# RWKV-6 attention and a SiLU MLP on one core: where block loads and one sum of weights stand in their queues

## The chip, the core and the metric

The kernel runs on one core of a Trainium2 chip. Such a core has a matrix engine (PE, TensorE), whose weight loads are shown apart as PEld, and a vector engine (DVE), a scalar engine (ACT), a general engine (POOL, GpSimd) and SyncE (SP), which here only issues transfers. Each engine takes its instructions in the order in which the program has them; an instruction whose semaphores are not yet set holds everything behind it on the same engine. The transfers themselves are carried out by 16 DMA engines.

The metric is the device time of one execution in microseconds. Before the change: 651.31 us, the median of 11 runs (649.45 to 654.97).

## The reference

A recurrent attention over 768 tokens, for 4 batches and 8 heads of 48 channels, and then a two-layer MLP on all 3072 tokens:

```python
for t in range(S):
    cur = np.einsum('bhd,bhe->bhde', u[None] * kt, vt)
    y[:, :, t] = np.einsum('bhd,bhde->bhe', rt, state + cur)
    state = wt[:, :, :, None] * state + np.einsum('bhd,bhe->bhde', kt, vt)
...
x = attn_out.transpose(0, 2, 1, 3).reshape(B * S, H * D)      # 3072 x 384
h = x @ w_in                                                  # 384 x 2048
g = h * (1.0 / (1.0 + np.exp(-h)))
out = g @ w_out                                               # 2048 x 384
```

r, k, v, w and u are 32-bit floats. The two weight matrices come as 64-bit floats, so that the kernel has to round them to 32 bits itself.

## The kernel before

**Units.** The sequence is cut into 6 chunks of 128 tokens, and the 4 batches into 2 pairs: 12 units, each 128 tokens of two batches. They are numbered from 0 in the code, so the third unit is `i = 2`, the fourth `i = 3`, the fifth `i = 4` and the sixth `i = 5`. A unit's attention is worked out in a tree of seven levels: at each level PE multiplies grown queries with grown keys (`score_products`, L527), VectorE copies the valid part into `score` under a mask (`keep_masked`, L537), and POOL and VectorE grow keys and queries for the next level (L491, L473, L595). Then the scores times the values give y (`y`, L665), the state is brought forward (`update`, L679 to L693), and y becomes x, the MLP's input (`dense_x`, L703 and L705, for the first two units, and `move_x`, ten transfers, later). A unit's MLP runs beside the attention of the units that follow it: eight `up` products with a Silu on ScalarE (L756, L762), then the product with w_out, plain for unit 0 (`down`, L775), and for the rest as seven products of halves (`quarter`, L819) with fewer multiplications, which need sums of the activations (`sums`, L801) and four sums of blocks of w_out, made once (`weight_sums`, L793). The last of these sums, `weight_sums(3)`, writes a block of w_out in place; the sixth of the seven products of unit 1 is its first reader.

**Loads of a unit.** The tokens of unit `i` stand in slot `i % 2` of `raw`. From the third unit on they come by `load_blocks` (L106): for each of w, k and r four calls, and each call issues four transfers of 32 tokens (16 or 32 KB), which makes 48 transfers for a unit. `load_values` (L119, L126) issues five more, `load_rk` (L90) four. All are issued by SyncE. The third unit's blocks are read first when VectorE transposes them (`turn`, L338).

**The diagonal.** A token's own term is not in the tree. POOL multiplies r, k and u (`bonus`), VectorE sums (`bonus_sum`, L415 and L419), and for `i >= 2` four small transfers on SyncE's queue put these sums into another order (`diag`, L425). ScalarE copies them (`bonus_spread`, L441 and L443), and VectorE writes them into `score` (L450).

**Rounding the weights.** The weights come in 16 pieces of 768 KB, 0 to 7 of w_in and 8 to 15 of w_out (`load_weight`, L178), into rooms that are used several times; pieces 0 to 5 are loaded at the start. The load of a later piece is issued right after the `join_weight` that has emptied its room: load 6 after piece 0, load 7 after piece 1, and so on to load 11 after piece 5; load 12 after piece 8, to load 15 after piece 11. A piece takes two steps on ScalarE for its upper bits (`head_weight`, L195 and L197), one for its lower ones into the buffer `p_w` (`tail_weight`, L203), two on VectorE (`join_weight`, L214 and L215) and a sum on POOL (`add_weight`, L227). The order of all this is written out by hand, in lists of steps that `do` emits one after the other. In the first of these, the second unit's tree begins beside the first unit's MLP; the third unit's blocks stand in it in three groups of four calls (`blocks[0:4]` is w, `[4:8]` k, `[8:12]` r).

**From the fourth unit on** the order comes from `mix(i)`: fourteen groups of steps of the attention, with the steps of the MLP of earlier units put between them (`ROOM` says how many behind each group). `mix` also deals out the loads for unit `i + 2`, with the values of unit `i + 1` in their middle, to the groups from the fourth on. For the fourth unit the loop adds `weight_sums(3)` at the end of group 4, which is the first burst of products (`burst`) and the masked copies of its first level (`keep_level`). The diagonal's four transfers stand in group 9 (`bonus_sum(i, 1)`), before `load_rk`.

Of the kernel before, what the change touches and what calls it, by code (L numbers as in the profile page):

```python
# [38 lines left out]
def kernel(  # L39
# [11 lines left out]
    nc = tc.nc  # L51
# [16 lines left out]
    NTOK = 2  # L68
# [650 lines left out]
    def both(fn, i, *args):  # L719
        return [(fn, i, b, *args) for b in range(NB)]  # L720

    def block_loads(i):
        return [(load_blocks, i, name, g) for name in "wkr" for g in range(4)]

    def mix(i):

        groups = [[*both(turn, i, "w"), (product, i, 0)],
                  [*both(turn, i, "k"), *both(turn, i, "r"), (odd_ones, i)], [(start_levels, i), (prepare_keys, i, 1)],
                  [(prepare, i, 1), *[(product, i, l) for l in range(1, NL)]],
                  [(burst, i, 1), (keep_level, i, 1)], [(keep_level, i, 2), (go_on, i, 2)],  # L730
                  [(prepare, i, 3), (reverse_v, i), (bonus, i, 0)],
                  [(burst, i, 3), (keep_level, i, 3), (bonus_sum, i, 0), (bonus, i, 1), (bonus, i, 2)],
                  [(keep_level, i, 4), (go_on, i, 4)],
                  [(prepare, i, 5), (bonus_sum, i, 1)] + ([(load_rk, i + 1)] if i + 1 < len(units) else []),
                  [(burst, i, 5), (keep_level, i, 5)], [(keep_level, i, 6), (go_on, i, 6), (bonus_spread, i), (bonus_write, i)],
                  both(turn_k, i), [*both(y_state, i), *both(y, i), *both(update, i), (move_x, i)]]

        loads = block_loads(i + NSLOT) if i + NSLOT < len(units) else []
        if i + 1 < len(units):
            loads.insert(len(loads) // 2, (load_values, i + 1))  # L740
        behind = groups[3:]
        for at, group in enumerate(behind):
            group += loads[at * len(loads) // len(behind):(at + 1) * len(loads) // len(behind)]
        return groups
# [89 lines left out]
    def ups(i):  # L834

        steps = [[(up, i, m)] for m in range(FC // 2)]
        for m in range(FH // 2 - 1):

            steps[FH // 2 + 1 + m].append((sums, i, m))
        steps[-1].append((sums, i, FH // 2 - 1))  # L840
        return steps

    def downs(i):
        return [[(quarter, i, x)] for x in range(7)]

    def do(*steps):
        for fn, *args in steps:
            fn(*args)
# [7 lines left out]
    def back(fn, i, *args):  # L856
# [8 lines left out]
    blocks = block_loads(2)  # L865
    others = {1: [(clear, 0), (beat, 6)], 2: [(turn, 1, 0, "r"), (head_weight, 0), (beat, 2)],
              3: [(turn, 1, 1, "r"), (head_weight, 1), (beat, 2)], 4: [(turn, 1, 1, "w"), (reverse_v, 0)],
              5: [(bonus_spread, 0), (bonus_write, 0), (turn, 1, 0, "w")], 6: [*both(turn_in, 1, "k"), *blocks[0:4], (tail_weight, 0)]}
    for l in range(1, NL):
        do((scores, 0, l), *[(grow_keys, 0, l + 1)] * (l + 1 < NL), *others[l])  # L870

    do((bonus, 1, 0), (bonus, 1, 1), (bonus, 1, 2), *both(y, 0), (turn_apart, 0), (join_weight, 0), (add_weight,),
       *blocks[4:8], (product, 1, 0), (tail_weight, 1), (turn, 1, 0, "k"), (join_weight, 1), (dense_x, 0, 0), (turn, 1, 1, "k"),
       (dense_x, 0, 1), (grow_queries, 1, 0), (odd_ones, 1), (tail_weight, 2), *both(turn_k, 0), (head_weight, 2),
       *blocks[8:12], (start_keys, 1, nc.gpsimd, True), (add_weight,), (up, 0, 0), (join_weight, 2),
       (start_keys, 1, nc.gpsimd, False), (add_weight,), (tail_weight, 3), (odd_keys, 1, 1), (head_weight, 3), (grow_keys, 1, 1),
       (scores, 1, 1, (join_weight, 3)), (add_weight,), (up, 0, 1), (tail_weight, 4), (grow_keys, 1, 2), (head_weight, 4),
       (up, 0, 2))


    others = {1: [], 2: [(bonus_sum, 1, 0), (bonus_sum, 1, 1), (load_rk, 2), *both(update, 0)],
              3: [(bonus_spread, 1), (reverse_v, 1), (clear, 1), (load_values, 2)]}

    def piece(i):
# [3 lines left out]
    for m in range(1, 4):  # L888
# [7 lines left out]
    blocks = block_loads(3)  # L896

    others = {0: [(up, 1, 1), (down, 0, 0, 0), *both(turn, 2, "k"), (product, 2, 0), (product, 2, 1)],
              1: [(up, 1, 2), *both(turn, 2, "r"), *[(product, 2, l) for l in range(2, NL)], *blocks[0:3]],
              2: [(down, 0, 0, 1), (odd_ones, 2), (start_keys, 2, nc.gpsimd, True), (grow_queries, 2, 0), *blocks[3:6]],  # L900
              3: [(up, 1, 3), (start_keys, 2, nc.gpsimd, False), (reverse_v, 2), *blocks[6:9]], 4: [(level, 2, 1), (up, 1, 4), *blocks[9:12]],
              5: [(down, 0, 0, 2), (up, 1, 5), (weight_sums, 0)]}
# [5 lines left out]
    blocks = block_loads(4)  # L908
# [10 lines left out]
    for i in range(3, len(units)):  # L919
        steps = downs(i - 2) + ups(i - 1)  # L920
        groups = mix(i)
        if i == NTOK + 1:

            groups[4].append((weight_sums, 3))
        for group, room in zip(groups, ROOM):
            do(*group)
            for step in steps[:room]:
                do(*step)
            steps = steps[room:]
# [32 lines left out]
```

## Time and profile before

| what | us |
|---|---|
| median of 11 runs | 651.31 |
| the profiled execution, and its span | 654.97, 653.2 |
| PE busy | 642.1 (98%) |
| PE weight loads busy | 580.8 (89%) |
| VectorE busy | 433.3 (66%) |
| POOL busy | 283.3 (43%) |
| ScalarE busy | 203.6 (31%) |
| PE busy from 28 to 70 us | 39.49 of 42.00 |
| PE busy from 140 to 150 us | 8.46 of 10.00 |
| PE busy from 150 to 183 us | 31.95 of 33.00 |
| PE busy from 183 to 234 us | 51.00 of 51.00 |

An entry of the page such as "L762 ACT ACTIVATE gt<-p_h" names the line of the code, the engine, the operation, and the tile written and the one read. In the timelines the first column is the start in us from the beginning of the span, the second the duration; what stands in square brackets is the idle time before it and what ended that. In the table of waits, the columns are the total in us, the number of waits and the longest. The clock is what the throttle granted to PE, 1.00 being full speed. The ends of matmuls are modelled, so that a busy PE isn't always a PE at its peak.

### The profile page before, as it was taken

How to read it: one execution, taken by the hardware profiler on the slowest of the kernel's cores; microseconds unless marked ns; L12 is line 12 of the kernel's file. 1: busy time of each engine (PE TensorE's matmuls, PEld its weight loads, DVE VectorE, ACT ScalarE, POOL GpSimd, SP SyncE). 2: the span in 40 equal slices, each digit the busy share in tenths (PEclk: the TensorE clock that was granted, in tenths of full speed). 3: DMA queues.
4: the chain of work that ended last, by engine and by line, in shares of the span. 5: the costliest groups of instructions: out<-in, count | busy, mean ns of one | idle time of the engine just before them, and what ended most of it. 6: DMA issues, size and time to landing. Idle time of an engine off the chain costs nothing.

```text
span 653.2 us, 12887 instructions
## 1 busy us (share of the span) xinstructions
PE 642.1 (98%) x4878; PEld 580.8 (89%) x4878; DVE 433.3 (66%) x737; ACT 203.6 (31%) x408; POOL 283.3 (43%) x356
## 2 busy tenths in 40 slices
PE   8999899999999999999999999999999999999998
PEld 7888776798899899899899899899989989989997
DVE  7879579888296586586686576586667765752031
ACT  5797782221221330331231231232222132131120
POOL 6898288565135334434416416416406505510000
PEclk9999899999999999999999999999999999999999
DMA  9956864544444513513513523432441022000000
GB/s 210 290 92 165 215 176 49 92 80 48 87 81 66 98 34 64 98 28 57 107 26 58 99 35 51 82 62 49 75 74 38 25 50 49 26 3 25 25 0 25
DMA packets 201134, 49.21 MB, mean 75 GB/s; under 512 B 188912, under 2 KB 195952, under 8 KB 201072
## 3 DMA queue, kind: packets, MB, share of 16 engines
q1 hardware_dynamic: 199488, 47.79, 36.0%
q8 instruction: 39, 0.64, 0.4%
q10 hardware_dynamic: 1584, 0.59, 0.4%
q14 instruction: 23, 0.19, 0.1%
HBM read 39.52 MB, written 4.72 MB: 68 GB/s over the span
## 4 chain that ended last, share of the span: by engine, by line
PE 90%; DMA 3%; SPq 2%; ACT 2%; DVE 1%; issue 1%; POOL 0%; POOLq 0%; ACTq 0%; DVEq 0%
PE p_h L756 35%; PE p_o L819 30%; PE p_sc L527 6%; PE p_m L527 4%; PE p_m L665 3%; PE p_m L775 3%; PE p_m L652 3%; PE p_m L350 2%; DMA w_out_sb<-in_moe_w_in_dram 1%; SPq L106 1%; PE p_m L639 1%; DMA w_out_sb<-in_moe_w_out_dram 1%; PE p_sc L679 1%; PE p_m L854 1%; PE p_m L703 1%
## 5 line engine op out<-in xcount | busy, mean ns | idle before, releaser
L756 PE MATMUL p_h<-xt,w_in_sb 128*128 128x256 f32 x1152 | 258.5, 382 | 1.8 <-ACT gt L762 1.1
L756 PEld LDWEIGHTS p_h<-xt,w_in_sb 128*128 128x128 f32 x1152 | 215.8, 190 | 33.8 <-ACT gt L762 1.3
L762 ACT ACTIVATE gt<-p_h 128x512 f32<-128x512 f32 x93 | 55.4, 596 | 222.6 <-PE p_h L756 222.4
L491 POOL TENSOR_TENSOR tk<-tk,tw 128x256 f32<-128x256 f32 x144 | 103.5, 742 | 21.9 <-ACT tk L461 15.0
L537 DVE COPY_PREDICATED score<-mask,p_sc 128x512 f32<-128x512 int8 x78 | 64.1, 885 | 60.4 <-PE p_sc L527 60.1
L819 PE MATMUL p_o<-w_out_sb,gt 128*128 128x192 f32 x528 | 90.5, 328 | 0.8 <-DVE w_out_sb L793 0.8
L819 PE MATMUL p_o<-own,temps 128*128 128x192 f32 x528 | 90.3, 328 | 0.7 <-DVE temps L828 0.7
L819 PEld LDWEIGHTS p_o<-own,temps 128*128 128x128 f32 x528 | 85.8, 190 | 2.1 <-DVE temps L828 1.0
L819 PEld LDWEIGHTS p_o<-w_out_sb,gt 128*128 128x128 f32 x528 | 85.8, 190 | 2.0 <-DVE w_out_sb L793 1.1
L684 POOL TENSOR_TENSOR state<-state,tw 128x512 f32<-128x512 f32 x16 | 19.7, 1253 | 119.7 <-PE p_m L652 119.7
L386 POOL TENSOR_TENSOR tw<-tw 128x256 f32<-128x256 f32 (+6 forms) x83 | 37.9, 456 | 56.6 <-DVE tw L338 52.7
L801 DVE TENSOR_TENSOR temps<-gt 128x256 f32<-128x256 f32 x88 | 44.1, 501 | 21.4 <-ACT gt L762 21.4
L461 ACT COPY tk<-tk 128x256 f32<-128x256 f32 x60 | 24.7, 412 | 81.5 <-PE p_sc L527 37.0
L527 PEld LDWEIGHTS p_sc<-tr,tk 48*128 48x128 f32 x640 | 39.2, 186 | 12.1 <-issue 8.4
L473 DVE TENSOR_TENSOR tr<-tr,tw 128x512 f32<-128x512 f32 x53 | 45.6, 861 | 3.3 <-POOL tk L491 1.1
L527 PE MATMUL p_sc<-tr,tk 48*128 48x128 f32 x640 | 47.1, 285 | 0.7 <-POOL tk L491 0.6
L408 POOL TENSOR_TENSOR ruk<-tokens_rk 128x768 f32<-128x768 f32 x10 | 18.6, 1861 | 66.7 <-DVE own_sums L415 66.7
L595 DVE TENSOR_TENSOR tr<-tr,tw 128x512 f32<-128x512 f32 x29 | 39.3, 1355 | 1.3
L537 DVE COPY_PREDICATED score<-mask,p_m 128x512 f32<-128x512 int8 x54 | 35.4, 706 | 0.0
L819 PE MATMUL p_o<-w_out_sb,temps 128*128 128x192 f32 x176 | 30.4, 326 | 0.0
L507 POOL TENSOR_TENSOR tk<-tk,tw 128x128 f32<-128x128 f32 x44 | 29.3, 701 | 1.7 <-ACT tk L497 1.7
L597 ACT COPY tr<-tr 128x512 f32<-128x512 f32 x29 | 18.4, 636 | 36.7 <-DVE tr L473 35.8
(144 smaller groups left out, 740.7 us busy)
## 6 DMA issues: line engine op xcount, KB each, us to landing
w_out_sb<-in_moe_w_in_dram SPq DMA_DIRECT2D x6, 768.0 KB, 7.1
tokens_rk<-in_r_dram SPq DMA_DIRECT2D x20, 192.0 KB, 3.4
tokens_rk<-in_k_dram SPq DMA_DIRECT2D x20, 192.0 KB, 3.9
w_out_sb<-in_moe_w_out_dram SPq DMA_DIRECT2D x4, 768.0 KB, 6.9
own<-in_moe_w_out_dram SPq DMA_DIRECT2D x4, 768.0 KB, 8.8
xt<-yt SPq DMA_DIRECT2D x60, 48.0 KB, 2.0
raw<-in_w_dram SPq DMA_DIRECT2D x80, 32.0 KB, 2.3
raw<-in_k_dram SPq DMA_DIRECT2D x80, 32.0 KB, 2.4
```

The costliest lines, as they stand in the source:

```text
L386: engine.tensor_tensor(out=up, in0=t[:, :, 0::2], in1=t[:, :, 1::2], op=ALU.mult)
L461: nc.scalar.copy(out=keys(i, X[(l + 1) % 2] * L + c, [4 * c, blocks], [c, 2], [1, c]), in_=keys(i, NP * L + c, [4 * c, blocks], [NP * L + ...
L473: nc.vector.tensor_tensor(out=odd, in0=odd, in1=tw[i][l][:, :, 0::2][:, :, :, None].to_broadcast([128, Q, L >> (l + 1), c]), op=ALU.mult)
L491: nc.gpsimd.tensor_tensor(out=out, in0=have, in1=odd_products(i, l, b, *blocks), op=ALU.mult)
L507: engine.tensor_tensor(out=keys(i, X[1] * L + 3 * b, [4, n], [1, 1]) if own else have, in0=have, in1=odd_products(i, 0, b, [4, n], skip=2 ...
L527: nc.tensor.matmul(bass.AP(tensor=s_p.tensor, offset=s_p.offset, ap=[s_p.ap[0], [apart * L // 2, 2], [1, L // 2]]), lhsT=tk[i][rows, X[l % ...
L537: nc.vector.copy_predicated(out=dst, mask=masks[l][:, :, None].to_broadcast([128, NB, NP, ni, c]), data=sc[e].rearrange("p (b q) (i c) -> ...
L595: nc.vector.tensor_tensor(out=new[:, :, :, 1, :], in0=old[:, :, :, 1, :], in1=tw[i][l][:, :, 0::2][:, :, :, None].to_broadcast([128, Q, L ...
L756: nc.tensor.matmul(p_h[:, a, :], lhsT=w_in_sb[:, c, f * 128:(f + 1) * 128], rhs=xt[i][:, c, :], start=(c == 0), stop=(c == KC - 1))
L762: nc.scalar.activation(out=gt[i, m], in_=p_h, func=AF.Silu)
L801: nc.vector.tensor_tensor(out=out, in0=one, in1=two, op=op)
L819: nc.tensor.matmul(p, lhsT=left(f), rhs=right[:, f, :], start=(f == 0), stop=(f == FH - 1))
```

## The change

Nothing is computed differently, and no instruction is added or dropped; three things change their place.

- The third unit's k blocks move from behind the first `add_weight` to behind `join_weight(2)`, and its r blocks from there to behind `up(0, 3)` in the first round of the loop over `m` below (`others[1]`).
- For the fourth unit alone (`i = 3`, `NTOK` is 2) the loads for the sixth unit and the values of the fifth are dealt out to the groups from number 10 on, where it was number 3.
- `weight_sums(3)` is put in as the second step of group 4, between the burst and the masked copies, where it was the last.

```diff
         loads = block_loads(i + NSLOT) if i + NSLOT < len(units) else []
         if i + 1 < len(units):
             loads.insert(len(loads) // 2, (load_values, i + 1))
-        behind = groups[3:]
+
+        behind = groups[3 if i > NTOK + 1 else 10:]
         for at, group in enumerate(behind):
             group += loads[at * len(loads) // len(behind):(at + 1) * len(loads) // len(behind)]
         return groups
...
     do((bonus, 1, 0), (bonus, 1, 1), (bonus, 1, 2), *both(y, 0), (turn_apart, 0), (join_weight, 0), (add_weight,),
-       *blocks[4:8], (product, 1, 0), (tail_weight, 1), (turn, 1, 0, "k"), (join_weight, 1), (dense_x, 0, 0), (turn, 1, 1, "k"),
+       (product, 1, 0), (tail_weight, 1), (turn, 1, 0, "k"), (join_weight, 1), (dense_x, 0, 0), (turn, 1, 1, "k"),
        (dense_x, 0, 1), (grow_queries, 1, 0), (odd_ones, 1), (tail_weight, 2), *both(turn_k, 0), (head_weight, 2),
-       *blocks[8:12], (start_keys, 1, nc.gpsimd, True), (add_weight,), (up, 0, 0), (join_weight, 2),
+       (start_keys, 1, nc.gpsimd, True), (add_weight,), (up, 0, 0), (join_weight, 2), *blocks[4:8],
        (start_keys, 1, nc.gpsimd, False), (add_weight,), (tail_weight, 3), (odd_keys, 1, 1), (head_weight, 3), (grow_keys, 1, 1),
...
-    others = {1: [], 2: [(bonus_sum, 1, 0), (bonus_sum, 1, 1), (load_rk, 2), *both(update, 0)],
+    others = {1: blocks[8:12], 2: [(bonus_sum, 1, 0), (bonus_sum, 1, 1), (load_rk, 2), *both(update, 0)],
               3: [(bonus_spread, 1), (reverse_v, 1), (clear, 1), (load_values, 2)]}
...
         if i == NTOK + 1:
 
-            groups[4].append((weight_sums, 3))
+            groups[4].insert(1, (weight_sums, 3))
```

## The prediction

> **What bounds the kernel now.** I began with the engine shares and the slices of the page.
>
> ```profile
> PE 642.1 (98%) x4878; PEld 580.8 (89%) x4878; DVE 433.3 (66%) x737; ACT 203.6 (31%) x408; POOL 283.3 (43%) x356
> PEclk9999899999999999999999999999999999999999
> ```
>
> TensorE (PE) is the bound; from 183 us its busy time in the table of stretches is 51.00 of every 51 us, so nothing is left there. What can be won lies in PE's idle time before 183 us, and in slice 5 (65 to 82 us), the one with a lower clock. Next, the waits of PE itself, longest first:
>
> ```profile
> PE p_m L665 <- ACT score L556: 2.3, 1, 2.3
> ...
> PE p_h L756 <- ACT gt L762: 1.1, 1, 1.1
> PE p_o L819 <- DVE w_out_sb L793: 0.8, 1, 0.8
> ...
> PE p_o L819 <- DVE temps L828: 0.7, 1, 0.7
> ```
>
> To see what is behind the first, ScalarE's timeline and SyncE's (start, duration, what):
>
> ```profile
> 60.94 1.48 ACT L365 COPY raw<-zero 128x1536 f32<-128x1536 f32 x1
> 67.06 0.90 ACT L195 ACTIVATE temps<-w_out_sb 128x768 bf16<-128x768 bf16 x1 [4.64 <-DMA w_out_sb<-in_moe_w_out_dram]
> ...
> 70.13 0.75 ACT L556 COPY score<-p_sc 64x256 f32<-64x256 f32 x2
> ```
> ```profile
> 39.65 0.38 SPq L178 DMA_DIRECT2D w_out_sb<-in_moe_w_in_dram  x1
> 40.14 10.13 SPq L106 DMA_DIRECT2D raw<-in_k_dram  x16
> 50.38 0.39 SPq L178 DMA_DIRECT2D w_out_sb<-in_moe_w_in_dram  x1
> 50.81 8.63 SPq L106 DMA_DIRECT2D raw<-in_r_dram  x16
> 59.97 0.90 SPq L178 DMA_DIRECT2D w_out_sb<-in_moe_w_out_dram  x2
> ```
>
> Weight load 8 (counting from 0) is issued at 59.97 and lands at 67.03, because loads 7 and 8 stand behind 16 block transfers each. Their rooms had long been free: DVE's L215 of piece 1 ended at 35.81, of piece 2 at 39.22. ScalarE waits 4.64 us in order, the copy of the score behind it is late, and PE stands from 68.28 to 70.54. The idle time isn't its whole price; the granted clock (the column after busy time) in half-microsecond stretches:
>
> ```profile
> 70.50:71.00 0.50, 0.46 (x8) 1.00 1.30 227
> ...
> 72.50:73.00 0.50, 0.50 (x8) 0.50 0.77 136
> ...
> 74.50:75.00 0.50, 0.50 (x5) 0.50 0.07 20
> ...
> 75.50:76.00 0.50, 0.50 (x7) 1.00 0.78 162
> ```
>
> Last, VectorE at the second place and SyncE at the third:
>
> ```profile
> 144.97 2.46 DVE L537 COPY_PREDICATED score<-mask,p_sc 128x512 f32<-128x512 int8 x2 [0.74 <-PE p_sc L527]
> 147.22 2.18 DVE L793 TENSOR_TENSOR w_out_sb<-w_out_sb,own 128x1536 f32<-128x1536 f32 x1
> ```
> ```profile
> 171.99 2.20 SPq L126 DMA_DIRECT2D vq<-in_v_dram  x4
> 174.29 2.44 SPq L425 DMA_DIRECT2D diag<-own_sums  x4
> ```
>
> The sum of weights ends at 149.41, and PE, done at 148.63, starts the product that reads it at 149.46. The diagonal's sums were ready at 163.38 (L419), but its four transfers stood on SyncE's queue until 174.29; they land at 177.89, ScalarE copies them, the next Silu is late, and PE stands from 178.30 to 179.35.
>
> **Part 1, the third unit's blocks.** Nothing is added or removed; 16 k transfers pass behind weight loads 7 and 8, and 16 r transfers behind loads 9 and 10. On SyncE a weight load takes 0.49 us (39.65 to 40.14), so loads 6, 7, 8 go at 39.65, 40.14, 40.63, all after their releases. The k blocks follow to 41.1 + 10.1 = 51.2, loads 9 and 10 at 51.3 and 51.8 (their pieces' L215 ended at 43.2 and 48.2), the r blocks to 52.2 + 8.6 = 60.8, load 11 at 60.8 (it was issued by 63.5). The blocks are first read at 79.55; 19 us hide their delay, and loads 12 to 15, bound by later pieces, don't move back.
>
> Three weight loads in a row at 39.65 aren't in the trace; nearest is the four in a row from 59.97, whose first lands in 7.06 us and whose slowest landing is 12.8. Even with 12.8, load 8 is there at 53.4, and ScalarE wants it at 62.42. The other side: load 6, wanted at 50.90, shares the engines. If three took three times the 4.88 of load 6 alone, it would land at 54.3, 3.4 us late; ScalarE's idle spots until 60.56 (0.35 + 0.27 + 0.76) and the slack below take it up, up to some 0.1 us. I take zero, as the first of the four landed first.
>
> ScalarE then goes on at 62.42. From its wait's end to the end of the score's copy it needs 70.88 - 67.06 = 3.82 us, so the copy ends at 66.2; VectorE's part of the score ends at 67.02. PE ends its work at 68.28, so the wait is gone with 1.3 us to spare: **2.26 us**. The half clock: start of L665 to start of L628 took 2.42 us against 1.90 for the same step of the first unit (30.47 to 32.37); on to L703 1.01 against 0.62; L703 itself 3.54 against 2.94. Together 0.52 + 0.39 + 0.60 = **1.51 us**. Bounds of part 1: 2.26, if the clock's share isn't won, and 3.77. I take 3.77. Behind it ScalarE, VectorE and the weights' pieces are chained to PE's products and come forward with it.
>
> The trace's row is a stall of 2.26 us and then about 3.5 us at clock 0.50. The Trainium skill (TensorE: Matmul & The Clock Gate, "Why this matters for your kernels") puts the limit for an idle gap at about 3 us, one idle window of 3.4 us; by this, so short a stall wouldn't cost any clock and removing it would win 2.26, 647.2 in all. The same page ("What's actually happening") has the window running freely, which would make this share vary from run to run. The row decides the forecast.
>
> **Part 2, the last sum of weights.** One 128x1536 instruction goes ahead of two masked copies. VectorE is free at 144.2 after the third product's sum, and its inputs are long ready. Four such sums took 1.75 to 2.59 us, so it ends by 146.0 to 146.8, before 148.63: **0.83 us** won. Queued behind it: the copies, now to about 148.8 (at the slowest 149.2, was 147.33), and the two sums of L828 for the next product, to 149.4 (was 149.87). PE reads none of this before 151.3, when the accumulator of that product is wanted again. Without the free 0.74 us there and that gap, the cost would be up to the 1.9 us by which the copies are late.
>
> **Part 3, the sixth unit's loads.** Before, 48 block and 5 value transfers were spread over eleven groups of the fourth unit; now they follow the diagonal's four and the four of the next r and k. On SyncE, in times of before: the fourth unit's last outputs go by 158, then the queue stands idle until 163.4, the diagonal takes 2.44 and lands near 167.7 (last issue + 1.8), 10 us ahead. The Silu behind it isn't held: **1.05 us**. What's late next: r and k 2.7 us to 168.7; two groups of 12 blocks at 0.52 us to 181.2; values 2.6 and 8 blocks 4.1 to 187.9; the ten moves of x 6.3 to 194.2 (was 195.04); 16 blocks 8.2 to 202.4, against 199.22. So the queue is 3.2 us late, 4.2 as PE is 1.05 earlier. In the fifth unit the diagonal then lands near 221.3 + 4.2 = 225.5; ScalarE asks for it at 225.24, and may be held until its next Silu has to end at 230.39, some 3.5 us. No stall, and the queue's 7 idle us from 230.4 (it waits for x until 237.47) take the delay up. Bounds: 1.05 down to a loss, see the rivals.
>
> **Sum.** 3.77 + 0.83 + 1.05 = 5.65 us. The profiled execution has a span of 653.2 within its 654.97; it becomes 647.55 within 649.3. It is 3.66 above the median of 651.31, and nothing shows which stretch was longer in it; I take the saving off the median: **645.7 us**. The remaining 0.71 us stall at 140.25 hangs on VectorE's own chain and stays.
>
> **Rivals.**
> (1) The clock's share isn't won, as it falls differently in other executions: 651.31 - 4.14 = 647.2. For it: stalls of 0.7 to 1.1 us elsewhere show no drop. Against: the drop is there in this one.
> (2) The first wait is only replaced: loads 6 to 8 delay each other, or the score is late from elsewhere. Parts 2 and 3 remain, 651.31 - 1.88 = 649.4. Against: VectorE's 67.02 and the 9 us between 53.4 and 62.42.
> (3) Part 2 or 3 gives nothing: 646.5 or 646.7.
> (4) Slower: the 48 gathered block transfers fill the queue. At the 0.73 us each of 87.11 (11.61 for 16) instead of 0.52, SyncE is 10 us later still, the fifth unit's diagonal lands near 235.6, its Silu ends at 237.3 instead of by 230.39, and PE loses 6.9 us and then 1.5 of clock. 651.31 - 4.6 + 8.4 = 655.1. It decides from about 0.6 us per transfer, where 3.5 us of slack is used up. Against: 0.49 us at 195 and at 179.
>
> **How the numbers follow.** Forecast 0.60, (1) 0.17, (2) 0.11, (3) 0.05, (4) 0.07. A measurement can tell about 0.3% from no change, 1.95 us: faster is below 649.36, slower above 653.26. Forecast, (1) and (3) are faster, (2) lies on the bound and is halved: faster 0.87, same 0.06, slower 0.07. The range goes down to 644.0 (the 0.71 stall won too, and a median that moves by 1, as its neighbours 650.83 to 651.84 do) and up to 649.4, rival (2).
>
> **What would show it.** In the profile after: loads 6 to 8 issued together near 40 us; no ScalarE wait on weights near 62 us, no PE wait at L665, clock 1.00 from 70 to 76; L793 ahead of L537, no PE wait on it; the diagonal issued before the blocks of unit six, no PE wait on L762. The forecast is wrong if a PE wait of over 1 us appears in the fifth unit, or a weight load holds ScalarE elsewhere.

## The result, and the profile after

| | before | after |
|---|---|---|
| median, us | 650.58 (63 runs) | 647.86 (17 runs) |
| lowest, highest | 648.79, 715.09 | 647.41, 648.66 |
| profiled execution, its span | 654.97, 653.2 | 648.22, 646.4 |
| PE waits at the three places, profiled | 2.3, 0.8, 1.1 | none |

The ratio is 0.9954 with a 95% interval of 0.9942 to 0.9966, that is 3.0 us (2.2 to 3.8) of 650.6; it compares means of fast executions, without the one at 715.09 us, and the two medians are 2.7 us apart. The direction and the mechanisms are those of the forecast; the gain is about half of the 5.65 us that it expected. The two profiled spans, on the other hand, differ by 6.8 us, more than the forecast. This gap between 6.8 and 3.0 is what the experiments had to explain.

First the page of the changed kernel (engine shares, and the granted clock by slices), then PE's waits:

```profile
PE 638.8 (99%) x4878; PEld 578.4 (89%) x4878; DVE 434.1 (67%) x737; ACT 204.1 (32%) x408; POOL 283.0 (44%) x356
PEclk9999999999999999999999999999999999999999
```
```profile
PE p_m L855 <- POOL ident masks.py:199: 1.4, 1, 1.4
PE p_h L757 <- POOL tk L507: 0.7, 1, 0.7
...
PE p_o L820 <- DVE temps L829: 0.4, 1, 0.4
```

PE is busy 3.3 us less, of which the half clock, 3.4 us long, accounts for some 1.7, and the waits for the score, for the sum of weights and for the Silu are gone. (Lines behind 741 have moved by one.) The first place, on SyncE's queue, and then on ScalarE and in PE's clock:

```profile
40.58 1.19 SPq L178 DMA_DIRECT2D w_out_sb<-in_moe_w_in_dram  x2
41.87 0.43 SPq L178 DMA_DIRECT2D w_out_sb<-in_moe_w_out_dram  x1
42.38 12.64 SPq L106 DMA_DIRECT2D raw<-in_k_dram  x16
55.13 0.39 SPq L178 DMA_DIRECT2D w_out_sb<-in_moe_w_out_dram  x1
```
```profile
62.26 0.92 ACT L195 ACTIVATE temps<-w_out_sb 128x768 bf16<-128x768 bf16 x1
```
```profile
72.00:74.00 2.00, 2.00 (x34) 1.00 1.29 230
```

Loads 6, 7 and 8 leave together near 41 us, and ScalarE takes up load 8 without a wait (it had stood for 4.64 us). The blocks behind them were slower than forecast: the 16 k blocks took 12.64 us where 10.1 was expected, and load 11, behind the r blocks, left at 66.97 instead of 60.8. ScalarE waited for none of the later weight loads. The second place, VectorE and then PE:

```profile
139.82 1.75 DVE L794 TENSOR_TENSOR w_out_sb<-w_out_sb,own 128x1536 f32<-128x1536 f32 x1
141.49 2.45 DVE L537 COPY_PREDICATED score<-mask,p_sc 128x512 f32<-128x512 int8 x2
```
```profile
144.14 2.76 PE L820 MATMUL p_o<-w_out_sb,gt 128*128 128x192 f32 x16
```

The third, with the next unit's diagonal, the one that had to bear the delay:

```profile
157.53 2.45 SPq L425 DMA_DIRECT2D diag<-own_sums  x4
...
162.84 8.97 SPq L106 DMA_DIRECT2D raw<-in_w_dram  x16
...
215.53 2.44 SPq L425 DMA_DIRECT2D diag<-own_sums  x4
```
```profile
219.21 0.84 ACT L443 COPY both_b<-diag 32x16 f32<-32x16 f32 x4 [0.73 <-DMA diag<-own_sums]
```

The fifth unit's diagonal is now what ScalarE waits for, 0.73 us, but PE isn't held.

Because idle time is only counted between modelled ends, I compare the two profiled executions by the starts of the same instruction:

| start of | before | after | gained by then | at this place | forecast |
|---|---|---|---|---|---|
| first `up` of the second unit | 78.30 | 74.41 | 3.89 | 3.89 | 3.77 |
| fourth product of halves of unit 1 | 140.96 | 136.64 | 4.32 | 0.43 | 0 |
| sixth product, behind the sum of weights | 149.46 | 144.14 | 5.32 | 1.00 | 0.83 |
| last `up` before 183 us | 179.35 | 172.71 | 6.64 | 1.32 | 1.05 |
| end of the span | 653.2 | 646.4 | 6.8 | 0.2 | 0 |

So against the execution that it was made from, each of the three terms was right to 0.3 us. The 0.43 us at the fourth product was not forecast: the wait there, 0.71 us before, was expected to stay and is 0.38 after. The change didn't do this, as the kernel before has 0.4 there too in its second profile, shown next.

### The profile page after: what moved, and what is told of

The parts are those of the page before. It is cut to its first block, busy times and chain, and to the rows that moved or that the text cites. A ratio compares the mean times of both kernels' runs of the same rounds, so it can differ in the third digit from the quotient of the medians.

```text
span 646.4 us, 12889 instructions
## 1 busy us (share of the span) xinstructions
PE 638.8 (99%) x4878; PEld 578.4 (89%) x4878; DVE 434.1 (67%) x737; ACT 204.1 (32%) x408; POOL 283.0 (44%) x356
## 4 chain that ended last, share of the span: by engine, by line
PE 94%; DMA 2%; DVE 1%; POOL 1%; ACT 1%; issue 0%; SPq 0%; ACTq 0%; DVEq 0%; POOLq 0%
PE p_h L757 39%; PE p_o L820 31%; PE p_sc L527 6%; PE p_m L527 4%; PE p_m L776 3%; PE p_m L665 3%; PE p_m L652 3%; DMA raw<-in_r_dram 2%; PE p_m L639 1%; PE p_sc L679 1%; PE p_m L703 0%; DVE score L450 0%; POOL tk L491 0%; POOL w_in_sb L227 0%; PE p_o L527 0%
## 5 line engine op out<-in xcount | busy, mean ns | idle before, releaser
L491 POOL TENSOR_TENSOR tk<-tk,tw 128x256 f32<-128x256 f32 x144 | 102.8, 737 | 23.4 <-ACT tk L461 16.4
L820 PE MATMUL p_o<-own,temps 128*128 128x192 f32 x528 | 90.3, 328 | 0.4 <-DVE temps L829 0.4
L820 PE MATMUL p_o<-w_out_sb,gt 128*128 128x192 f32 x528 | 90.4, 328 | 0.0
L820 PEld LDWEIGHTS p_o<-own,temps 128*128 128x128 f32 x528 | 85.8, 190 | 1.8 <-DVE temps L829 0.7
L820 PEld LDWEIGHTS p_o<-w_out_sb,gt 128*128 128x128 f32 x528 | 85.9, 190 | 0.9 <-issue 0.4
L386 POOL TENSOR_TENSOR tw<-tw 128x256 f32<-128x256 f32 (+6 forms) x83 | 39.3, 473 | 54.5 <-DVE tw L338 50.6
L473 DVE TENSOR_TENSOR tr<-tr,tw 128x512 f32<-128x512 f32 x53 | 46.2, 872 | 3.9 <-POOL tw L386 1.4
L595 DVE TENSOR_TENSOR tr<-tr,tw 128x512 f32<-128x512 f32 x29 | 40.0, 1378 | 1.3
L820 PE MATMUL p_o<-w_out_sb,temps 128*128 128x192 f32 x176 | 30.4, 326 | 0.0
L829 DVE TENSOR_TENSOR partial<-p_o,partial 128x192 f32<-128x192 f32 x33 | 11.7, 354 | 27.6 <-PE p_o L820 27.6
```

The source lines that it names most:

```text
L386: engine.tensor_tensor(out=up, in0=t[:, :, 0::2], in1=t[:, :, 1::2], op=ALU.mult)
L473: nc.vector.tensor_tensor(out=odd, in0=odd, in1=tw[i][l][:, :, 0::2][:, :, :, None].to_broadcast([128, Q, L >> (l + 1), c]), op=ALU.mult)
L491: nc.gpsimd.tensor_tensor(out=out, in0=have, in1=odd_products(i, l, b, *blocks), op=ALU.mult)
L595: nc.vector.tensor_tensor(out=new[:, :, :, 1, :], in0=old[:, :, :, 1, :], in1=tw[i][l][:, :, 0::2][:, :, :, None].to_broadcast([128, Q, L ...
L820: nc.tensor.matmul(p, lhsT=left(f), rhs=right[:, f, :], start=(f == 0), stop=(f == FH - 1))
```

## The experiments

**The kernel before once more.** The kernel is unchanged. Theory V was that the first stall varies from execution to execution, G that the gain is given back somewhere.

> The kernel before, unchanged, profiled once more. Measured for the whole change: 647.86 against 650.58 us, ratio 0.9954, some 3.0 us, where the profiled executions differ by 6.8 us of span (653.2 to 646.4). Theory V (the first stall varies): the profiled execution of before was a long one at the first place; in others the weight load lands earlier or the clock doesn't drop. Then this span is near 650.6 - 1.8 = 648.8, PE's wait at L665 is below 1.5 us or the clock stays at 1.00 from 70 to 76 us, and the waits at L819 and L756 are again 0.8 and 1.1. Theory G (given back): every execution of before has the 2.3 us wait and the half clock, and the change loses some 2.6 us in a place that PE's waits don't show; then this span is near 653.

Measured: 650.18 us, span 648.3. ScalarE's timeline and PE's waits of this execution:

```profile
64.60 0.91 ACT L195 ACTIVATE temps<-w_out_sb 128x768 bf16<-128x768 bf16 x1 [2.24 <-DMA w_out_sb<-in_moe_w_out_dram]
```
```profile
PE p_o L819 <- DVE w_out_sb L793: 0.8, 1, 0.8
...
PE p_h L756 <- ACT gt L762: 0.5, 1, 0.5
PE p_o L819 <- DVE temps L828: 0.4, 1, 0.4
```

Load 8 was issued at 60.04, as in the first profile (59.97), but took 4.5 us to land, not 7.06. ScalarE's wait of 2.24 us is wholly taken up by the slack between it and PE: no wait at L665, full clock. The third place costs 0.5, not 1.1. This execution has 4.9 us less of span than the first profile, with the same program. V holds, G falls.

**The three parts alone.** Each is one hunk of the diff shown above, the rest as before.

> Part 1 alone (the third unit's k and r blocks behind the weight loads). Theory V: 3.0 us less parts 2 and 3 (0.83 + 1.05), so 1.1 us, ratio about 0.998. Theory G: the forecast 3.77, ratio 0.994, and the three parts alone sum to 5.6 us, much more than the whole. In the profile both expect no wait at L665 and full clock, and the waits at L819 (0.8) and L756 (1.1) as before.

> Part 2 alone (the last sum of weights in front of the masked copies). Both theories: 0.83 us, ratio 0.9987. Its profile still has the first place as before and is a further look at it: V expects the wait at L665 or the clock's drop to differ from the 2.3 us and 0.50 of the first profile, G expects the same.

> Part 3 alone (the sixth unit's loads behind the fourth's diagonal). Both theories: 1.05 us, ratio 0.9984, no wait of the fifth unit's diagonal on PE. If the gathered loads did harm, a PE wait at L756 in the fifth unit (some 50 us after the fourth's) and a ratio over 1. A third look at the first place, as part 2.

| part alone | median, us (before 650.64) | ratio, 95% interval | PE waits of its profile at the three places |
|---|---|---|---|
| 1 | 650.13 | 0.9987 (0.9975 to 1.0) | none, 0.8, 0.4 |
| 2 | 649.99 | 0.9992 (0.9977 to 1.0007) | 1.8, none, 2.0 |
| 3 | 649.57 | 0.9979 (0.9959 to 1.0) | 1.7, 0.8, none |

Each part removes its wait. By the ratios none is worth more than some 1.4 us, and the three add up to about 2.7 us, near the whole's 3.0. None of the three intervals excludes no change. Part 1 is worth 0.85 us, not 3.77: its interval excludes the 0.994 of theory G. Parts 2 and 3 leave the first place as it was, so that their profiles show it twice more: there PE stood for 1.8 and 1.7 us, at full clock. From part 2's profile, the waits, and the clock after the wait at L665:

```profile
PE p_h L756 <- ACT gt L762: 2.0, 1, 2.0
PE p_m L665 <- ACT score L556: 1.8, 1, 1.8
```
```profile
70.00:72.00 2.00, 2.00 (x36) 1.00 1.16 265
72.00:74.00 2.00, 2.00 (x29) 1.00 1.21 190
```

The wait at L756 is the longest seen in this group. SyncE's queue, busy without a pause, sets when the diagonal leaves; what PE wins ahead of it by part 2, it mostly waits longer at the diagonal. (Against the repeated profile of the kernel before, the queue's ten moves of x start 1.8 us later, 136.98 against 135.15, and the diagonal leaves 2.2 us later, while PE, with the wait for the sum gone, is only 0.7 us later when it comes to the diagonal.)

**Parts 2 and 3 without part 1.**

> Parts 2 and 3 without part 1. SyncE's queue sets when the diagonal leaves in the kernel before, so what part 2 wins ahead of it is eaten by the wait at L756, which grew from 0.4 to 1.1 us in the other looks to 2.0 with part 2 alone. Together they should win more than the sum of what they win alone: by start to start times of the two first profiles 1.0 for part 2 and 0.8 to 1.3 for part 3, so 1.8 to 2.3 us, ratio 0.9965 to 0.9972, with no PE wait at L793 or L756. If they only add as measured (0.5 and 1.4), 1.9: that can't be told apart by time, and the waits decide. The first place is as in the kernel before, and its wait varies again.

Measured: 648.33 against 650.55 us, ratio 0.9959 (0.9943 to 0.9974), 2.7 us by the means and 2.2 by the medians; 1.8 to 2.3 was expected, and the interval (1.7 to 3.7 us) also holds the 1.9 of a plain sum. No wait is left at L793 or L756. In its profile load 8 landed 4.5 us after issue and the first place had no PE wait, so its span of 646.6 is nearly that of the whole change. The whole's ratio of 0.9954 lies within its interval: on top of parts 2 and 3, part 1 adds nothing that the medians can tell.

**Only the r blocks.** Part 1 without its first move:

```diff
        (dense_x, 0, 1), (grow_queries, 1, 0), (odd_ones, 1), (tail_weight, 2), *both(turn_k, 0), (head_weight, 2),
-       *blocks[8:12], (start_keys, 1, nc.gpsimd, True), (add_weight,), (up, 0, 0), (join_weight, 2),
+       (start_keys, 1, nc.gpsimd, True), (add_weight,), (up, 0, 0), (join_weight, 2),
...
-    others = {1: [], 2: [(bonus_sum, 1, 0), (bonus_sum, 1, 1), (load_rk, 2), *both(update, 0)],
+    others = {1: blocks[8:12], 2: [(bonus_sum, 1, 0), (bonus_sum, 1, 1), (load_rk, 2), *both(update, 0)],
```

> Part 1 without its k blocks: only the r blocks move, so load 8 is issued near 50.5 instead of 60. If load 8's landing is all that matters, PE's wait at L665 is gone and the ratio is that of part 1, about 0.9987; if the k blocks' move matters (load 7, wanted at 56.1), a ScalarE wait on a weight load shows near 55 us.

Measured: 650.01 against 650.55 us, ratio 0.9989 (0.9978 to 1.0), the same as part 1. SyncE and ScalarE:

```profile
49.94 0.93 SPq L178 DMA_DIRECT2D w_out_sb<-in_moe_w_out_dram  x2
```
```profile
62.59 0.92 ACT L195 ACTIVATE temps<-w_out_sb 128x768 bf16<-128x768 bf16 x1
```

Load 8 leaves at 49.94, and ScalarE finds it at 62.59 without a wait; it takes up load 7 at 56.42, also without one. In this profile the move of the k blocks wasn't needed.

**Load 8 later.** Two kernels, made from the one before by one edit of the table that says after which piece a load is issued; in the first load 8 stands behind load 9, in the second behind 9, 10 and 11:

```diff
+    due[3] += due.pop(2)
+    due[2] = []
```
```diff
+    due[5] += due.pop(2)
+    due[2] = []
```

> The kernel before, with weight load 8 issued right behind load 9 instead of in front of it, so that its landing comes some 2 to 4 us later and PE's wait at L665 grows from 0 to 2.3 us (four looks so far) to 3.5 to 6 us. Theory H: a longer stall always brings the half clock, so clock 0.50 for some 3.5 us after it, and the time rises by the added stall and 1.5 us more: 654 to 657, ratio 1.006 to 1.010. Rival: the drop in the first profile had nothing to do with the stall; then the clock stays at 1.00 here and the time rises by the added stall alone, 652.5 to 655.

> The kernel before, with load 8 issued last of the four loads near 60 us (behind 9, 10 and 11). With load 8 behind load 9 alone, it landed near 66.7 and PE stood for 1.75 us at full clock. By the landings of the third and fourth load in the other looks (8 to 10 us after issue), it lands here near 69.5 to 72, ScalarE waits 7 to 9.5 us and PE 4.5 to 7. Theory H (a stall of over some 2 us brings the half clock): clock 0.50 for about 3.5 us after it, and a ratio of 1.009 to 1.013. Rival: the clock stays at 1.00, and the ratio is that of the stall alone, 1.006 to 1.010; the profile's clock decides.

The first expectation failed in its size: load 8 landed at 66.75, some 6.4 us after issue, hardly later than where it goes first, and PE stood for 1.75 us at full clock. The ratio is 1.0027 (1.0007 to 1.0046), below both theories. The second is clear: ratio 1.0134 (1.0105 to 1.0162), 8.7 us. Its waits, and its clock:

```profile
PE p_m L667 <- ACT score L558: 6.1, 1, 6.1
```
```profile
72.00:72.50 0.50, 0.00 (x0) 0.93 1.39 203
72.50:73.00 0.50, 0.00 (x0) 0.50 1.40 171
...
79.00:79.50 0.50, 0.50 (x5) 0.74 0.17 33
```

The long stall brings the half clock in all four executions (mean clock 0.991 to 0.995), in the profiled one for 6.8 us, twice what H expected. That a longer stall always brings it, as the first expectation had H say, is not so: in the first kernel three of ten executions were at 654.61 to 656.09 us, and these are the three with a mean clock of 0.997; the other seven have 0.999 or 1.000 and 650.23 to 653.00.

**The same, with PE kept busy.** The kernel with load 8 behind load 9, and:

```diff
-    do((scores, 1, NL - 1), (join_weight, 8), (add_weight,), (up, 0, 7), *both(y, 1), (turn_apart, 1),
+    do((scores, 1, NL - 1), (join_weight, 8), (add_weight,), (up, 0, 7), (beat, 32), *both(y, 1), (turn_apart, 1),
```

> As the kernel with load 8 behind load 9, and 32 transposes of a constant tile on PE (4.2 us by 0.13 us each at full clock) before the products that wait, their result unused. If PE's idleness brings the half clock and transposes count as work, the clock stays at 1.00 and the time is 1.5 us below that kernel's. If transposes don't count, or PE isn't what the clock follows, the clock falls as there and the times are equal. The added work fits in the stall; where the stall is shorter, it costs the rest of 4.2 us.

Measured: 652.92 against 650.55 us, ratio 1.0034 (1.0023 to 1.0046), not 1.5 us below the kernel without the transposes (652.15) but 0.8 above. The premise failed first: without the transposes, most executions keep the full clock, so there was little to win. The transposes took 3.66 us; that this is longer than the stall of most executions would explain the 0.8 us, and isn't shown. In six executions the mean clock was 0.999 or 1.000, and none went over 653.69, where the kernel without them reached 656.09. That fits PE's clock counting transposes as work, but six executions against three drops in ten don't prove it.

**An earlier second product.** From the changed kernel, to remove its last PE wait in this region (L820, 0.4 us):

```diff
-        for group, room in zip(groups, ROOM):
+        for group, room in zip(groups, (2, 0, *ROOM[2:]) if i == NTOK + 1 else ROOM):
```

> The changed kernel, with the second of unit 1's seven products put in front of VectorE's k and r transposes of the fourth unit instead of behind them (two steps behind group 0, none behind group 1), so that its sum no longer waits for them. The wait of PE left in the profile after at L820 (0.4 us) should go: 0.4 to 0.5 us less than the changed kernel, which is about what five rounds can tell. Rival: the transposes, 0.3 us later, hold the fourth unit's first burst, and nothing is won.

> The changed kernel unchanged, on the chip of the next one: ratio 0.9954 again, and no execution above 649.5.

The changed kernel gave 0.9954 again (0.9939 to 0.9969), 647.92 us with none over 648.48. The new one gave 651.00, ratio 1.0006 (0.9991 to 1.002): 3.1 us worse than the changed kernel. Nothing is won, as the rival said, and more is lost, but not for the rival's reason: the burst's first products start without a wait at 138.78, and its second ones wait for POOL. PE, POOL and PE's clock in it:

```profile
141.62 1.16 PE L527 MATMUL p_m<-tr,tk 48*128 48x128 f32 x16 [1.66 <-POOL tk L491]
142.71 4.55 PE L820 MATMUL p_o<-own,temps 128*128 128x192 f32 x16
```
```profile
138.60 2.96 POOL L491 TENSOR_TENSOR tk<-tk,tw 128x256 f32<-128x256 f32 x2 [0.56 <-ACT tk L461]
```
```profile
143.00:143.50 0.50, 0.50 (x5) 0.92 0.30 45
143.50:144.00 0.50, 0.50 (x3) 0.50 0.37 43
...
146.50:147.00 0.50, 0.50 (x4) 0.67 0.33 34
```

The wait of 0.4 us is gone, but POOL's pair of key products takes 2.96 us, PE waits 1.66 us for it, and then the 16 products of L820 take 4.55 us at half clock instead of 2.87. In the changed kernel the same pair took 1.44 us:

```profile
138.46 1.44 POOL L491 TENSOR_TENSOR tk<-tk,tw 128x256 f32<-128x256 f32 x2 [0.56 <-ACT tk L461]
139.87 3.92 POOL L386 TENSOR_TENSOR tw<-tw 128x256 f32<-128x256 f32 x6
```

There it is the work after it, the six products of L386, that takes 3.92 us; without the sum beside them, in the kernel just tried, they take 2.35. In each of the two kernels the slow group is the one that runs beside VectorE's sum of weights (139.82 to 141.57, and 139.22 to 140.97).

**The sum between the copies.** The same kernel, with the sum moved behind the first of the two masked copies:

```diff
-            groups[4].insert(1, (weight_sums, 3))
+            groups[4][1:2] = [(lambda: keep_masked(i, 1, 0, made[i, 1]),), (weight_sums, 3), (lambda: keep_masked(i, 1, 1, made[i, 1]),)]
```

> The kernel with the earlier second product, and the last sum of weights between the two masked copies of the burst's first level instead of in front of them. In the kernel with the earlier second product POOL's pair at L491 took 2.96 us from 138.60, where it took 1.44 in the changed kernel, VectorE's sum ran from 139.22 to 140.97 beside it, and PE waited 1.66 us for POOL and fell to half clock. Theory P (the sum holds POOL up while both run): here the sum starts about 141, after L491; the pair takes 1.4 to 1.5 us again, the wait of 1.66 and the half clock go, the sum is done by 143, in time for the product that reads it, and the time is that of the changed kernel or up to 0.5 us less, 647.4 to 647.9. Rival (POOL was slow for another reason, and the burst came too early): the wait at L527 stays at 1 us or more and the time is near 650. If the sum is now too late for its product, a wait at L794 appears again.

Measured: 647.54 us (five runs, 647.27 to 647.64) against 650.90, ratio 0.995 (0.9936 to 0.9964), span 645.8. POOL and VectorE:

```profile
138.19 1.44 POOL L491 TENSOR_TENSOR tk<-tk,tw 128x256 f32<-128x256 f32 x2 [0.56 <-ACT tk L461]
139.57 3.93 POOL L386 TENSOR_TENSOR tw<-tw 128x256 f32<-128x256 f32 x6
```
```profile
140.69 1.78 DVE L794 TENSOR_TENSOR w_out_sb<-w_out_sb,own 128x1536 f32<-128x1536 f32 x1
```

Theory P holds: the pair is back at 1.44 us, and the slow group is again the one beside the sum. PE has no wait left from 76 to 183 us. This is the lowest median of all, 0.4 us below the changed kernel's 647.92; the intervals of the two ratios overlap, so that the step from one to the other is seen in the profile and not proved by the times.

## Why the forecast was right in direction and twice too large

**What bounds the kernel, and the three places.** Right. PE is the bound, the three waits were the only ones that the change reaches, and each is gone in the profile after, and in the profile of each part alone.

**The terms.** Against the execution that they were read from, they were right: 3.77 forecast and 3.89 found at the first place, 0.83 and 1.00, 1.05 and 1.32. The forecast used the idle time before the late instruction, and that came out 0.2 to 0.3 us short of the difference in starts at the second and third place. After part 3 the fifth unit's diagonal was issued 5.6 us later, as seen from PE (215.53 against 216.54 less the 6.64 that PE was ahead by), where 4.2 was forecast, and the slack took it up. That is 1.4 us in the direction of rival (4), the gathered transfers (the first 16 took 0.56 us each, where 0.52 was forecast), but short of costing PE anything.

**The step that failed** is the one that went from this execution to the median: "It is 3.66 above the median, and nothing shows which stretch was longer in it; I take the saving off the median". The surplus was, nearly all of it, in the very stalls that the change removes: against the second profile of the same kernel, 4.9 us longer in span, it had 2.26 us of wait and 1.5 of half clock more at the first place, and 0.6 at the third. So it was counted as a gain in executions that had less of it or none. Load 8, issued first of four near 60 us, took 7.06, 4.5, 6.5, 6.0 and 4.5 us to land in the five profiles that keep its order, and PE waited 2.3, 0, 1.8, 1.7 and 0 us. The third place had 1.1 us in the first profile, 0.5, 0.4 and 0.4 in the three others where the queue ahead of it and the second place were as before, and 0.2 or none in the kernels that issue load 8 later. And the half clock was the exception: of the 81 executions of the kernel before that ran beside the experiments, four have a mean clock of 0.997 or lower, and they took 652.75, 653.39, 654.35 and 656.74 us. The profiled execution, with a clock of 0.997 and 654.97 us, was of this kind. The mis-sized term is part 1: 3.77 in the sum, 0.85 by the ratio when alone (interval 0 to 1.6), and not measurably different from 0 on top of the two others.

**The rivals.** Rival (1), the half clock not won, came nearest in time (647.2, where 647.86 was measured), partly because the larger set of runs has a median 0.7 us below the 651.31 that it was taken off; its saving of 4.1 us kept the stall of 2.26 us, which is the longest of the five. Rival (2), parts 2 and 3 alone, is what the medians look like, 1.88 us forecast and 2.7 measured for these two (2.2 by the medians), though not for its reason: the first wait wasn't replaced; two of the five profiles that could have it don't, and only one has the half clock.

**What part 1 may bring** is a narrower spread. The kernel before ranges from 648.8 to 656.7 us (leaving out one of 715), with part 1 alone from 649.15 to 651.02, and the changed kernel, 26 executions of two sessions, from 647.41 to 648.66. That part 1 is needed for the narrow spread of the whole isn't shown: the five executions of parts 2 and 3 without it lie between 647.55 and 648.63, though the profiled one still had ScalarE wait 2.0 us for load 8.

**What the forecast didn't see** is what the sum of weights does to POOL. It named VectorE's copies behind the sum, but not POOL's work beside it, which becomes some 1.5 us slower. The price itself isn't new, it moves with the sum: in the kernel before, the sum (147.22 to 149.40) ran beside four later products of L491, which took 4.01 us there and 2.62 in the changed kernel.

```profile
146.50 4.01 POOL L491 TENSOR_TENSOR tk<-tk,tw 128x256 f32<-128x256 f32 x4
```
```profile
143.74 2.62 POOL L491 TENSOR_TENSOR tk<-tk,tw 128x256 f32<-128x256 f32 x4
```

In the changed kernel six products of L386 bear it, and nobody waits for them; with the sum 0.6 us earlier it is on PE's path.

## What to carry to other kernels

Before a stall is taken off a median, see whether the median has it: a profiled execution above the median, and its mean clock, say that some of its stalls may be its own, and one or two more profiles of the same program tell which. Here the waits on transfers varied (0 to 2.3 us at the first place), and the wait on VectorE's sum hardly did (0.8 to 0.9 us at the second place in every profile that keeps it), so the two kinds of gain didn't carry over to the median alike. And when an instruction is moved on one engine, look at what runs beside it on the others, as POOL's products here, as well as at what is queued behind it.

## What the runs showed of the hardware

- **The half clock comes in steps of 3.42 us.** Read from the stretches that it fills in part: 71.83 to 75.25 in the kernel before, 143.42 to 146.83 in the kernel with the earlier product, and 72.43 to 79.26 (twice 3.42) after the stall of 6.1 us. The Trainium skill (TensorE: Matmul & The Clock Gate, "What's actually happening") gives a free-running window of 3413 ns, and these durations agree. Its limit for an idle gap of about 3 us ("Why this matters for your kernels") doesn't: stalls of 1.66 and 2.26 us brought the half clock, while stalls of 1.7, 1.75, 1.8 and 2.0 us did not. Length alone doesn't decide it in this range. That the position of the stall in the window does would fit, and isn't shown: in both cases with a drop the 3.42 us that end where the half clock begins hold nearly the whole stall (2.1 of 2.26 us, 1.6 of 1.66).
- **A stall can be paid twice.** The 1.66 us wait in the kernel with the earlier product also cost some 1.7 us of half speed (4.55 against 2.87 for the next 16 products), and 9 of its 12 executions have a clock of 0.997 or less. The other three, at full clock, took 649.54 to 650.22 us, the nine 650.72 to 652.83.
- **A large sum on VectorE all but stops POOL.** In three kernels a VectorE sum of two 128x1536 operands ran for 1.75 to 1.78 us beside POOL's products of two operands, and the POOL group took 1.5 to 1.6 us more (2.96 against 1.44, and 3.92 and 3.93 against 2.35). In the kernel before, a POOL group took 1.4 us more beside the same sum (4.01 against 2.62), and the sum itself took 2.18. The Trainium skill (GPSIMD Engine Reference, "1. Specifications") states that GpSimd shares its SBUF interfaces with VectorE and contends with instructions that have two SBUF inputs; the runs agree and give the size.
- **One transfer, one place in the queue, 4.5 to 7.1 us to land.** A load of 768 KB, first of four in a row, issued at 59.9 to 60.9 us, varied by this much from one profile to another. What sets it stays open; 32 block transfers and three more loads were on the same queue each time.
